# A cached-attention decode kernel: separate room for the K and V buffers, and an MLP cut into pieces between the head groups

## The chip, the cores and the metric

One core of a Trainium2 chip. The metric is the device time of one execution in microseconds, the median of several executions. All runs told here were in the fast state, with the same granted TensorE clock (0.52 on average in every kernel). A profile adds the span of one profiled execution, which lies 1 to 3 us under the median of the timed runs. In the lines of the profile PE is TensorE, PEld its weight loads, DVE VectorE, ACT ScalarE, POOL GpSimd and SP SyncE; the DMA share is the mean busy share of the core's 16 DMA engines.

## The reference

One decode step: attention over a long cache plus an MLP, both fed from the same normalised input, and a residual.

```python
# B=8, H=32, Sk=4096, Dh=128, D=576, F=4608; everything bf16
xn = _layernorm(x)
q  = (xn @ wq)                                  # 8 x 4096, 32 heads of 128
p  = softmax(einsum("bhqd,bhkd->bhqk", q, k_cache) * Dh**-0.5)
o  = einsum("bhqk,bhkd->bhqd", p, v_cache) @ wo
y  = _layernorm(xn)
m  = einsum("bsf,fd->bsd", gelu(einsum("bsd,df->bsf", y, w1) + b1), w2) + b2
return x + o + m
```

The caches K and V are 268 MB each; the four weights are 4.7 to 5.3 MB each. Everything is read once.

## The kernel before

It runs in stages: layer norms and query product; MLP; 128 groups of two heads (8 batches x 16 pairs); final product. Each group loads 2 MB of K from SP's queue and 2 MB of V from ACT's queue into three buffers each. Of the 32 blocks of keys per head, 12 are scored on PE (transposed against an identity, copied by ACT, multiplied by the query), 20 on VectorE (product with the broadcast query, four halving adds, a reduction). ACT takes the exponential, PE multiplies by V.

```python
wo_sb = const.tile([P, H, D], BF16, name="wo_sb")
nc.gpsimd.dma_start(out=wo_sb, in_=A_wo.rearrange("(h p) d -> p h d", p=P))

with tc.tile_pool(name="wq_pool", bufs=1) as wq_pool, ...:      # released before the MLP
    for ci, (d0, dn) in enumerate(d_chunks):                    # 4 blocks of 128 rows, one of 64
        nc.scalar.dma_start(out=wq_sb[:dn, ci, :], in_=A_wq[d0:d0 + dn, :])
    # ... layer norms, query product, q transposed ...

with tc.tile_pool(name="mlp_w", bufs=1) as mlp_w, ...:          # takes wq's room
    # ... w1 (5 loads), then w2, on GpSimd's queue ...
    b1T = mlp_w.tile([P, FC], BF16, name="b1T")                 # 4608 elements of 2 bytes
    nc.gpsimd.dma_start(out=b1T, in_=B_b1.rearrange("(c p) -> p c", p=P))
    for fc in range(FC):                                        # 36 x 5 matmuls, weights = w1
        ...
    # ... bias, tanh gelu, 72 matmuls with w2 moving, sum with x and b2 -> mlpx_sb

with tc.tile_pool(name="kv_pool", bufs=KV_BUFS) as kv_pool, \
     tc.tile_pool(name="kt_pool", bufs=3) as kt_pool, \
     tc.tile_pool(name="pr_pool", bufs=2) as pr_pool, ...:      # takes the MLP weights' room
    for b in range(B):
        for hg in range(NHG):
            nc.sync.dma_start(out=k_sb, in_=A_k_cache[...])     # 2 MB
            nc.scalar.dma_start(out=v_sb, in_=A_v_cache[...])   # 2 MB
            # ... PE transposes, kT copies, scores; VectorE prod, adds, reduce; exp; PV ...

# the end: normalise, then O (8 columns) stationary and wo moving
for h in range(H):
    for (n0, nn) in ncols:
        nc.tensor.matmul(acc[:, n0:n0 + nn], lhsT=On[:, h * B:(h + 1) * B], rhs=wo_sb[:, h, n0:n0 + nn], ...)
nc.vector.tensor_tensor(out=fin, in0=acc, in1=mlpx_sb, op=ALU.add)
```

The softmax here doesn't subtract the row's maximum and nothing guards it: scores larger than these inputs give would overflow.

Of the kernel before, what the change touches and what calls it, by code (L numbers as in the profile page):

```python
# [12 lines left out]
ALU = mybir.AluOpType  # L13
ACT = mybir.ActivationFunctionType
# [4 lines left out]
X_PE = int(os.environ.get("MB_X", "12"))  # L19
HG = int(os.environ.get("MB_HG", "2"))  # L20
KV_BUFS = int(os.environ.get("MB_KVB", "3"))


@with_exitstack
def kernel(
# [19 lines left out]
    assert Dh == P, Dh  # L45
    assert S % P == 0
    C = S // P
    assert F % P == 0
    FC = F // P
    d_chunks = []  # L50
    d0 = 0
    while d0 < D:
        n = min(P, D - d0)
        d_chunks.append((d0, n))
        d0 += n
    NDC = len(d_chunks)
    HD_TOTAL = H * Dh
    N512 = 512
    scale = float(Dh) ** -0.5
# [19 lines left out]
    )  # L79
    ident = const.tile([P, P], BF16, name="ident")  # L80
    make_identity(nc, ident)
    ones_f = const.tile([P, P], FP32, name="ones_f")
    nc.vector.memset(ones_f, 1.0)
    eps_col = const.tile([P, 1], FP32, name="eps_col")
# [2 lines left out]
    x8 = const.tile([B, D], BF16, name="x8")  # L87
    nc.sync.dma_start(out=x8[:], in_=x2)

    xT = const.tile([P, NDC, B], BF16, name="xT")  # L90
    yT = const.tile([P, NDC, B], BF16, name="yT")
    q8 = const.tile([B, HD_TOTAL], BF16, name="q8")
    qT = const.tile([P, H, B], BF16, name="qT")

    wo_sb = const.tile([P, H, D], BF16, name="wo_sb")
    nc.gpsimd.dma_start(out=wo_sb, in_=A_wo.rearrange("(h p) d -> p h d", p=P))

    with tc.tile_pool(name="wq_pool", bufs=1) as wq_pool, \
         tc.tile_pool(name="ln_sb", bufs=2) as ln_sb, \
         tc.tile_pool(name="ln_ps", bufs=2, space=bass.MemoryType.PSUM) as ln_ps:  # L100
        wq_sb = wq_pool.tile([P, NDC, HD_TOTAL], BF16, name="wq_sb")
        for ci, (d0, dn) in enumerate(d_chunks):
# [24 lines left out]
        y8 = const.tile([B, D], BF16, name="y8")  # L127
        layernorm(xn8, y8, "b")

        for src, dstT in ((xn8, xT), (y8, yT)):  # L130
            for ci, (d0, dn) in enumerate(d_chunks):
                tpx = ln_ps.tile([P, B], FP32, name="tpx")
                nc.tensor.matmul(tpx[:dn, :], lhsT=src[:, d0:d0 + dn], rhs=ident_b[:, :], start=True, stop=True)
                nc.vector.tensor_copy(out=dstT[:dn, ci, :], in_=tpx[:dn, :])

        nq = (HD_TOTAL + N512 - 1) // N512
        for j in range(nq):
            n0 = j * N512
            nn = min(N512, HD_TOTAL - n0)
            qps = ln_ps.tile([B, N512], FP32, name="qps")  # L140
            for ci, (d0, dn) in enumerate(d_chunks):
                nc.tensor.matmul(  # L142
                    qps[:, :nn], lhsT=xT[:dn, ci, :], rhs=wq_sb[:dn, ci, n0:n0 + nn],
                    start=(ci == 0), stop=(ci == NDC - 1),
                )
            nc.scalar.activation(out=q8[:, n0:n0 + nn], in_=qps[:, :nn], func=ACT.Copy, scale=scale)  # L146
        for h in range(H):
            tq = ln_ps.tile([P, B], FP32, name="tq")
            nc.tensor.matmul(tq[:, :], lhsT=q8[:, h * P:(h + 1) * P], rhs=ident_b[:, :], start=True, stop=True)  # L149
            nc.vector.tensor_copy(out=qT[:, h, :], in_=tq[:, :])  # L150

    sel = const.tile([B, B, P], BF16, name="sel")
    nc.vector.tensor_copy(out=sel, in_=ident_b[:, :].unsqueeze(2).to_broadcast([B, B, P]))

    mlpx_sb = const.tile([B, D], FP32, name="mlpx_sb")
    with tc.tile_pool(name="mlp_w", bufs=1) as mlp_w, \
         tc.tile_pool(name="mlp_sb", bufs=2) as mlp_sb, \
         tc.tile_pool(name="mlp_ps", bufs=1, space=bass.MemoryType.PSUM) as mlp_ps:
        w1_sb = mlp_w.tile([P, NDC, F], BF16, name="w1_sb")
        for ci, (d0, dn) in enumerate(d_chunks):  # L160
            nc.gpsimd.dma_start(out=w1_sb[:dn, ci, :], in_=B_w1[d0:d0 + dn, :])
        w2_sb = mlp_w.tile([P, FC, D], BF16, name="w2_sb")
        nc.gpsimd.dma_start(out=w2_sb, in_=B_w2.rearrange("(c p) d -> p c d", p=P))
        b1T = mlp_w.tile([P, FC], BF16, name="b1T")
        nc.gpsimd.dma_start(out=b1T, in_=B_b1.rearrange("(c p) -> p c", p=P))
        b2_bc = mlp_w.tile([B, D], BF16, name="b2_bc")
        nc.gpsimd.dma_start(out=b2_bc, in_=B_b2.partition_broadcast(B))

        hT_ps = mlp_ps.tile([P, FC, B], FP32, name="hT_ps")
        for fc in range(FC):  # L170
            for ci, (d0, dn) in enumerate(d_chunks):
                nc.tensor.matmul(  # L172
                    hT_ps[:, fc, :],
                    lhsT=w1_sb[:dn, ci, fc * P:(fc + 1) * P],
                    rhs=yT[:dn, ci, :],
                    start=(ci == 0), stop=(ci == NDC - 1),
                )
        x1 = mlp_sb.tile([P, FC, B], FP32, name="x1")
        nc.vector.tensor_tensor(  # L179
            out=x1, in0=hT_ps, in1=b1T[:, :].unsqueeze(2).to_broadcast([P, FC, B]), op=ALU.add,  # L180
        )
        t1 = mlp_sb.tile([P, FC, B], FP32, name="t1")
        nc.vector.tensor_tensor(out=t1, in0=x1, in1=x1, op=ALU.mult)
        nc.vector.tensor_scalar(out=t1, in0=t1, scalar1=0.044715, scalar2=1.0, op0=ALU.mult, op1=ALU.add)
        nc.vector.tensor_tensor(out=t1, in0=t1, in1=x1, op=ALU.mult)
        t2 = mlp_sb.tile([P, FC, B], FP32, name="t2")
        nc.scalar.activation(out=t2, in_=t1, func=ACT.Tanh, scale=GELU_C)
        nc.vector.tensor_scalar(out=t2, in0=t2, scalar1=1.0, scalar2=0.5, op0=ALU.add, op1=ALU.mult)
        hT_sb = mlp_sb.tile([P, FC, B], BF16, name="hT_sb")
        nc.vector.tensor_tensor(out=hT_sb, in0=t2, in1=x1, op=ALU.mult)  # L190

        mlp_ps2 = mlp_ps.tile([B, D], FP32, name="mlp_ps2")
        ncols = []
        c0 = 0
        while c0 < D:
            ncols.append((c0, min(N512, D - c0)))
            c0 += N512
        for fc in range(FC):
            for (n0, nn) in ncols:
                nc.tensor.matmul(  # L200
                    mlp_ps2[:, n0:n0 + nn], lhsT=hT_sb[:, fc, :], rhs=w2_sb[:, fc, n0:n0 + nn],
                    start=(fc == 0), stop=(fc == FC - 1),
                )
        tmpx = mlp_sb.tile([B, D], FP32, name="tmpx")
        nc.vector.tensor_tensor(out=tmpx, in0=x8, in1=b2_bc, op=ALU.add)
        nc.vector.tensor_tensor(out=mlpx_sb, in0=mlp_ps2, in1=tmpx, op=ALU.add)

    O_sb = const.tile([P, H, B], FP32, name="O_sb")
    Epart = const.tile([P, H, B], FP32, name="Epart")

    with tc.tile_pool(name="kv_pool", bufs=KV_BUFS) as kv_pool, \
         tc.tile_pool(name="kt_pool", bufs=3) as kt_pool, \
         tc.tile_pool(name="pr_pool", bufs=2) as pr_pool, \
         tc.tile_pool(name="e_pool", bufs=3) as e_pool, \
         tc.tile_pool(name="qb_pool", bufs=2) as qb_pool, \
         tc.tile_pool(name="ps_tp", bufs=2, space=bass.MemoryType.PSUM) as ps_tp, \
         tc.tile_pool(name="ps_sc", bufs=2, space=bass.MemoryType.PSUM) as ps_sc, \
         tc.tile_pool(name="ps_o", bufs=2, space=bass.MemoryType.PSUM) as ps_o, \
         tc.tile_pool(name="ps_qb", bufs=1, space=bass.MemoryType.PSUM) as ps_qb:

        def make_qb(b):
            qb_sb = qb_pool.tile([P, HD_TOTAL], BF16, name="qb_sb")
# [6 lines left out]
                nc.scalar.activation(out=qb_sb[:, n0:n0 + nn], in_=qb_ps[:, :nn], func=ACT.Copy)  # L229
            return qb_sb  # L230

        qb_cur = make_qb(0)
        for b in range(B):
            qb_next = None
            for hg in range(NHG):
# [9 lines left out]

                if hg == NHG // 2 and b + 1 < B:
                    qb_next = make_qb(b + 1)

                E = e_pool.tile([P, HG, C], BF16, name="E")
                kT = kt_pool.tile([P, HG, XB, 512], BF16, name="kT") if X > 0 else None  # L250
# [54 lines left out]
                    )  # L305
                for g in range(HG):
                    for c in range(C):
                        nc.tensor.matmul(  # L308
                            o_ps[:, g:g + 1], lhsT=v_sb[:, g, c, :], rhs=E[:, g, c:c + 1],
                            start=(c == 0), stop=(c == C - 1),  # L310
                        )
# [2 lines left out]
                )  # L314
            if qb_next is not None:
                qb_cur = qb_next

    with tc.tile_pool(name="fin_sb", bufs=1) as fin_sb, \
         tc.tile_pool(name="fin_ps", bufs=1, space=bass.MemoryType.PSUM) as fin_ps:
# [5 lines left out]
        On = fin_sb.tile([P, H * B], BF16, name="On")  # L325
        nc.vector.tensor_tensor(out=On, in0=O_sb[:, :, :].rearrange("p h b -> p (h b)"), in1=recip, op=ALU.mult)

        acc = fin_ps.tile([B, D], FP32, name="acc")
        ncols = []
        c0 = 0  # L330
        while c0 < D:
            ncols.append((c0, min(N512, D - c0)))
            c0 += N512
        for h in range(H):
            for (n0, nn) in ncols:
                nc.tensor.matmul(  # L336
                    acc[:, n0:n0 + nn], lhsT=On[:, h * B:(h + 1) * B], rhs=wo_sb[:, h, n0:n0 + nn],
                    start=(h == 0), stop=(h == H - 1),
                )
        fin = fin_sb.tile([B, D], BF16, name="fin")  # L340
        nc.vector.tensor_tensor(out=fin, in0=acc, in1=mlpx_sb, op=ALU.add)
        nc.sync.dma_start(out=out2, in_=fin)


# [28 lines left out]
```

## Time and profile before

| what | value |
|---|---|
| time, median of 4 runs | 1392.62 us (1391.82 to 1392.92) |
| span of the profiled execution | 1391.1 us |
| bytes moved | 559.1 MB, 402 GB/s over the span |
| busy: PE, DVE, ACT | 58%, 61%, 40% |
| chain that ended last | DMA 63%, DVE 20%, PE 11%, ACT 3% |

Bytes divided by span is the first thing to work out: 402 GB/s on average against about 426 in the steady slices. The difference is what a change at the two ends can win, 5 to 6%. The other rows say that no engine is near its limit. The lines are in the prediction.

### The profile page before, as it was taken

The page shows a single profiled execution, that of the slowest core. Times are in us where ns is not written, and L with a number is a line of the kernel's source. Part 1 is how long each engine was busy: PE and PEld are TensorE (multiplying, and loading weights), DVE is VectorE, ACT ScalarE, POOL GpSimd, SP SyncE. Part 2 cuts the span into 40 slices and gives each one's busy share as a digit, 9 for nine tenths or more (in the row PEclk, how much of TensorE's full clock was granted, in tenths as well). Part 3 has the DMA queues.
Part 4 walks back from the last instruction along what each step waited for, and adds up shares of the span by engine and source line. Part 5 has one row for each costly group of instructions (what it writes and reads, how often), then busy time and mean ns, then how long its engine had stood idle before and what let it go on. Part 6 is the DMA issues. An engine that isn't in the chain of part 4 may idle for free.

```text
span 1391.1 us, 33564 instructions
## 1 busy us (share of the span) xinstructions
PE 802.0 (58%) x14800; PEld 670.3 (48%) x14800; DVE 850.2 (61%) x1604; ACT 551.4 (40%) x1485; POOL 9.6 (1%) x17
## 2 busy tenths in 40 slices
PE   4645565756566556655556555655556555555566
PEld 1324454545454545454545454555445545445454
DVE  2026657666657576666675766666666666666663
ACT  2213343534344434443444443443435443434342
POOL 1100000000000000000000000000000000000000
PEclk9565555555555555555555555555555555555556
DMA  7849999999999999999999999999999999999991
GB/s 272 307 191 426 426 425 426 425 426 426 425 426 420 425 423 426 415 425 426 418 425 426 419 426 419 427 425 414 425 424 419 426 419 426 423 421 424 417 426 65
DMA packets 73458, 559.12 MB, mean 402 GB/s; under 512 B 4424, under 2 KB 4448, under 8 KB 6624
## 3 DMA queue, kind: packets, MB, share of 16 engines
q10 hardware_dynamic: 35472, 273.16, 47.1%
q1 hardware_dynamic: 34848, 268.46, 45.7%
q0 software_dynamic: 2992, 15.35, 3.1%
q8 instruction: 115, 1.88, 0.5%
q14 instruction: 31, 0.25, 0.0%
HBM read 556.95 MB, written 0.01 MB: 400 GB/s over the span
## 4 chain that ended last, share of the span: by engine, by line
DMA 63%; DVE 20%; PE 11%; ACT 3%; issue 1%; ACTq 1%; POOL 0%; DVEq 0%; SPq 0%
DMA k_sb<-in_A_k_cache_dram 60%; DVE prod L287 9%; DVE prod L278 9%; PE o_ps L308 6%; DMA b1T<-in_B_b_dram 2%; PE tp L260 2%; DVE sc_ps L294 2%; ACT kT L264 2%; DMA wq_sb<-in_A_wq_dram 1%; ACT E L302 1%; PE qps L142 1%; PE acc L336 1%; PE mlp_ps L200 1%; ACTq L242 1%; ACT O_sb L312 0%
## 5 line engine op out<-in xcount | busy, mean ns | idle before, releaser
L278 DVE TENSOR_TENSOR prod<-k_sb,qb_sb 128x2560 bf16<-128x2560 bf16 x256 | 370.4, 1488 | 445.0 <-DMA k_sb<-in_A_k_cache_dram 445.0
L308 PE MATMUL o_ps<-E,v_sb 128*128 128x1 bf16 x8192 | 236.2, 165 | 463.7 <-ACT E L302 463.7
L264 ACT ACTIVATE kT<-tp 128x512 bf16<-128x512 f32 x768 | 442.4, 596 | 117.7 <-PE tp L260 85.5
L308 PEld LDWEIGHTS <-v_sb 128*128 128x128 bf16 x8192 | 243.1, 105 | 488.7 <-issue 488.7
L260 PE MATMUL tp<-ident,k_sb 128*128 128x128 bf16 x3072 | 440.7, 302 | 63.7 <-ACT kT L264 31.9
L287 DVE TENSOR_TENSOR prod<-prod 128x1280 bf16<-128x1280 bf16 (+3 forms) x1024 | 401.1, 463 | 0.1
L260 PEld LDWEIGHTS <-k_sb 128*128 128x128 bf16 x3072 | 291.6, 130 | 99.2 <-issue 59.6
L302 ACT ACTIVATE E<-sc_ps 128x32 bf16<-128x32 f32 x256 | 48.1, 193 | 474.3 <-DVE sc_ps L294 474.3
L269 PEld LDWEIGHTS <-kT 128*128 128x128 bf16 x3072 | 171.0, 116 | 53.2 <-ACT kT L264 53.1
L269 PE MATMUL sc_ps<-qT,kT 128*128 128x1 bf16 x3072 | 173.1, 172 | 5.1 <-ACT kT L264 0.2
L294 DVE TENSOR_REDUCE sc_ps<-prod 128x20 f32<-128x160 bf16 x256 | 82.8, 323 | 6.1 <-PE sc_ps L269 1.8
L312 ACT ACTIVATE O_sb<-o_ps 128x2 f32<-128x2 f32 x128 | 22.2, 174 | 156.9 <-PE o_ps L308 156.9
L228 PE MATMUL qb_ps<-q,sel 8*128 8x512 bf16 x64 | 37.0, 579 | 20.7 <-ACT qb_sb L229 20.6
L229 ACT ACTIVATE qb_sb<-qb_ps 128x512 bf16<-128x512 f32 x64 | 38.4, 599 | 26.0 <-DVE prod L278 16.0
L302 ACT ACTIVATION_READ_ACCUMULATOR E<-sc_ps 128x1 f32 x256 | 47.7, 198 | 0.0
L142 PE MATMUL qps<-wq_sb,xT 128*8 128x512 bf16 (+1 forms) x40 | 14.9, 486 | 10.7 <-DMA wq_sb<-in_A_wq_dram 10.7
L179 DVE TENSOR_TENSOR x<-hT_ps,b1T 128x288 f32<-128x288 f32 x1 | 0.5, 457 | 29.8 <-DMA b1T<-in_B_b_dram 29.8
L200 PE MATMUL mlp_ps<-w_sb,hT_sb 128*8 128x512 bf16 x72 | 10.7, 317 | 10.5 <-DVE hT_sb L190 10.5
L172 PEld LDWEIGHTS <-w_sb 128*128 128x128 bf16 (+1 forms) x180 | 10.5, 106 | 7.0 <-issue 5.4
L150 DVE CAST qT<-tq 128x8 bf16<-128x8 f32 x32 | 4.1, 162 | 15.0 <-PE tq L149 14.8
L146 ACT ACTIVATE q<-qps 8x512 bf16<-8x512 f32 x8 | 4.7, 587 | 21.0 <-PE qps L142 21.0
L200 PEld LDWEIGHTS <-hT_sb 128*8 128x8 bf16 x72 | 4.6, 94 | 16.3 <-DVE hT_sb L190 10.6
(56 smaller groups left out, 73.5 us busy)
## 6 DMA issues: line engine op xcount, KB each, us to landing
k_sb<-in_A_k_cache_dram SPq DMA_DIRECT2D x128, 2048.0 KB, 18.9
v_sb<-in_A_v_cache_dram ACTq DMA_DIRECT2D x128, 2048.0 KB, 17.3
w_sb<-in_B_w_dram POOLq DMA_DIRECT2D x1, 5184.0 KB, 31.2
wo_sb<-in_A_wo_dram POOLq DMA_DIRECT2D x1, 4608.0 KB, 26.1
w_sb<-in_B_w_dram POOLq DMA_DIRECT2D x4, 1152.0 KB, 9.0
wq_sb<-in_A_wq_dram ACTq DMA_DIRECT2D x4, 1024.0 KB, 9.5
w_sb<-in_B_w_dram POOLq DMA_DIRECT2D x1, 576.0 KB, 17.6
wq_sb<-in_A_wq_dram ACTq DMA_DIRECT2D x1, 512.0 KB, 17.5
```

The source lines that it names most:

```text
L142: nc.tensor.matmul(qps[:, :nn], lhsT=xT[:dn, ci, :], rhs=wq_sb[:dn, ci, n0:n0 + nn], start=(ci == 0), stop=(ci == NDC - 1),)
L200: nc.tensor.matmul(mlp_ps2[:, n0:n0 + nn], lhsT=hT_sb[:, fc, :], rhs=w2_sb[:, fc, n0:n0 + nn], start=(fc == 0), stop=(fc == FC - 1),)
L228: nc.tensor.matmul(qb_ps[:, :nn], lhsT=sel[:, b, :], rhs=q8[:, n0:n0 + nn], start=True, stop=True)
L229: nc.scalar.activation(out=qb_sb[:, n0:n0 + nn], in_=qb_ps[:, :nn], func=ACT.Copy)
L260: nc.tensor.matmul(tp[:, t * P:(t + 1) * P], lhsT=k_sb[:, g, c, :], rhs=ident[:, :], start=True, stop=True,)
L264: nc.scalar.activation(out=kT[:, g, blk, :], in_=tp[:, :], func=ACT.Copy)
L269: nc.tensor.matmul(sc_ps[:, g, c:c + 1], lhsT=kT[:, g, blk, t * P:(t + 1) * P], rhs=qT[:, h, b:b + 1], start=True, stop=True,)
L278: nc.vector.tensor_tensor(out=prod[:, g, :, :], in0=k_sb[:, g, X:C, :], in1=qb_cur[:, h * Dh:(h + 1) * Dh].unsqueeze(1).to_broadcast([P, R ...
L287: nc.vector.tensor_tensor(out=prod[:, g, :, 0:half], in0=prod[:, g, :, 0:half], in1=prod[:, g, :, half:width], op=ALU.add,)
L294: nc.vector.tensor_reduce(out=sc_ps[:, g, X:C], in_=prod[:, g, :, 0:width], axis=mybir.AxisListType.X, op=ALU.add,)
L302: nc.scalar.activation(out=E[:, g, :], in_=sc_ps[:, g, :], func=ACT.Exp, accum_out=Epart[:, h, b:b + 1],)
L308: nc.tensor.matmul(o_ps[:, g:g + 1], lhsT=v_sb[:, g, c, :], rhs=E[:, g, c:c + 1], start=(c == 0), stop=(c == C - 1),)
```

## The change

Its intent: start reading K and V at once, by giving their buffers room that no weight holds, and do the MLP in small pieces beside the loop, so that the weights take turns in one room on the other side of the memory.

```diff
+    w1_pool = tc.alloc_tile_pool(name="w1_pool", bufs=1, side="right")   # later w2, then wo, take this room
-    wo_sb = const.tile([P, H, D], BF16, name="wo_sb")
-    nc.gpsimd.dma_start(out=wo_sb, in_=A_wo.rearrange("(h p) d -> p h d", p=P))
+    nc.sync.dma_start(out=b1T, in_=B_b1.rearrange("(p c) -> p c", p=P))
+    nc.sync.dma_start(out=b2T[:, 0:NDC_FULL], in_=B_b2[0:D_FULL].rearrange("(c p) -> p c", p=P))
+    kv_pool = ctx.enter_context(tc.tile_pool(name="kv_pool", bufs=KV_BUFS))
+    wq_pool = tc.alloc_tile_pool(name="wq_pool", bufs=1, side="right")
... the whole MLP stage is removed ...
-         tc.tile_pool(name="kt_pool", bufs=3) as kt_pool, \
-         tc.tile_pool(name="pr_pool", bufs=2) as pr_pool, \
+    with tc.tile_pool(name="kt_pool", bufs=2) as kt_pool, \
+         tc.tile_pool(name="pr_pool", bufs=1) as pr_pool, \
+        def w1_unit(j):                       # 20 matmuls, 4 of 36 blocks of F
+            for i4 in range(4):
+                for ci, (d0, dn) in enumerate(d_chunks):
+                    nc.tensor.matmul(hps[:, i4, :],
+                        lhsT=w1s[:dn, ci, :].rearrange("k (p c) -> k c p", c=FC)[:, 4 * j + i4, :],
+                        rhs=yT[:dn, ci, :], ...)
... bias, gelu -> hT_sb; w2_unit(j): 20 matmuls with w2 stationary, added into finT ...
+        for j in range(FJ):                   # FJ = 9
+            group_events.setdefault(j + 2, []).append(("w1", j))
+        group_events.setdefault(W2_ISSUE_GROUP, []).append(("w2_issue", 0))    # 11, ACT's queue
+            group_events.setdefault(W2_START_GROUP + j, []).append(("w2", j))  # 14 and on
+        group_events.setdefault(W2_START_GROUP + FJ, []).append(("wo_issue", 0))  # 23, SP's queue
...
+                if gi == 0:                   # behind the first K load
+                    for ci, (d0, dn) in enumerate(d_chunks):
+                        nc.sync.dma_start(out=w1_sb[:dn, ci, :], in_=B_w1[d0:d0 + dn, :])
... at the end: wo stationary, 160 matmuls of 8 columns; sum with finT; 5 fp32 matmuls turn it to rows ...
-                    acc[:, n0:n0 + nn], lhsT=On[:, h * B:(h + 1) * B], rhs=wo_sb[:, h, n0:n0 + nn],
+                    att_ps[:dn, ci, :], lhsT=wo_sb[:, h, d0:d0 + dn], rhs=On[:, h * B:(h + 1) * B],
```

## The prediction

> **What bounds the kernel now.** I read the slices of the page first, then the chain that ended last, then busy time by stretch at the two ends, then the timeline around the waits.
>
> ```profile
> DMA  7849999999999999999999999999999999999991
> GB/s 272 307 191 426 426 425 426 425 426 426 425 426 420 425 423 426 415 425 426 418 425 426 419 426 419 427 425 414 425 424 419 426 419 426 423 421 424 417 426 65
> ...
> HBM read 556.95 MB, written 0.01 MB: 400 GB/s over the span
> ```
>
> One slice is 34.8 us. From the fourth slice on the transfers run flat at about 426 GB/s: the loop over K and V is bound by data movement, and every engine idles in it (VectorE, the busiest, 61%). Only the first three slices and the last are below that. A change that moves no fewer bytes can win only there.
>
> ```profile
> 38.31 32.82 DMA b1T<-in_B_b_dram
> ...
> 75.49 10.71 PE mlp_ps L200 x72
> 86.22 0.76 DVE mlpx_sb L206
> ...
> 87.50 22.58 DMA k_sb<-in_A_k_cache_dram
> ```
>
> The chain in order of time (start, length, what). A 9 KB bias holds the MLP until 71 us, the second MLP product takes 10.7 us, and only then does the first K load start, at 87: the K buffers lie in the room of the MLP weights and wait until these are done with. The columns below are stretch, length, busy time and count of PE, its weight loads, DVE, ACT and POOL, granted clock, DMA share, GB/s.
>
> ```profile
> 25.00:30.00 5.00, 5.00 (x17) 1.11 (x15) 0.00 (x0) 1.72 (x3) 0.00 (x0) 1.00 0.40 151
> 30.00:35.00 5.00, 4.60 (x24) 1.54 (x23) 1.00 (x8) 2.44 (x6) 1.21 (x3) 1.00 0.00 0
> ...
> 65.00:70.00 5.00, 0.00 (x0) 0.00 (x0) 0.00 (x0) 0.00 (x0) 0.00 (x0) 0.50 0.04 7
> 70.00:75.00 5.00, 0.00 (x0) 0.00 (x0) 2.58 (x7) 0.44 (x1) 0.00 (x0) 0.50 0.00 2
> 75.00:80.00 5.00, 4.51 (x23) 1.84 (x24) 0.43 (x1) 0.00 (x0) 0.00 (x0) 0.60 0.00 0
> 80.00:85.00 5.00, 5.00 (x43) 2.34 (x40) 0.00 (x0) 0.00 (x0) 0.00 (x0) 1.00 0.00 0
> ...
> 300.00:1300.00 1000.00, 579.36 (x11239) 502.11 (x11239) 654.34 (x1210) 418.22 (x1140) 0.00 (x0) 0.50 1.01 423
> ```
>
> The reader is to see two holes in the transfers, one around 30 us (the MLP weights wait for room that the query weights hold) and one from 65 to 87. From the page, the first three slices moved (272+307+191) x 34.8 us = 26.8 MB, which 426 GB/s would move in 62.9 us instead of 104.3: **about 41 us of transfer time are lost at the front.**
>
> **What the Trainium skill says.** "DMA: Bandwidth & Descriptors", section Specifications, gives 435 GB/s as the fabric ceiling; the steady 426 of this trace is 98% of it, so I count no further speed-up of the loop. The same page, "Issuing engines are not separate DMA queues": DMAs from any engine run on the same 16 DMA engines and interleave. So moving the weights from GpSimd's queue to SP and ACT wins nothing by itself, and prefetches from both share the 426 rather than add to it; in this trace two queues with 47.1% and 45.7% share it. The same page's rules for kernel authors: a strided last dimension becomes one descriptor per element. The bias load is one such (4,608 elements of 2 bytes) and took 32.8 us from issue to landing, behind the 5.3 MB of w2 in its queue; in 65 to 70 us DMA share is 4%, so its end is latency. "ScalarE: Activation LUTs", section "Table sets: the hidden batching unit": exp and tanh share a set. The trace agrees: only two table loads of 1.28 us, before the square root and before the tanh, none before the 256 exps. So tanh amid exps should reload nothing.
>
> **The change part by part.** (1) K and V buffers get their own room, so their loads have nothing to wait for but their issue. (2) The MLP is cut into 9 pieces per product and put between head groups: w1 loads behind the first K, its pieces run in groups 2 to 10; w2 takes w1's room at group 11, pieces in groups 14 to 22; wo takes w2's room at group 23. (3) The bias gets a layout of 128 rows of 72 bytes; b2 gets 576 two-byte elements, an eighth as many as b1 before. (4) The final product is turned round: wo becomes the stationary operand. (5) kT buffers go from 3 to 2, prod buffers from 2 to 1.
>
> Transfers: the bytes stay at 559.1 MB. Before, 20.7 MB had moved by 90 us (sum of the 5 us stretches), and 538.4 MB at 423 GB/s from there end at 1362.9; the stretch 1360 to 1365 with 159 GB/s says about 1362, so the account closes. After: start 2.5 us (before, 210 GB/s in the first 5 us is a start at 2.5), plus 559.1 / 423 = 1321.7, plus 3 us for the last row block of wq and of w1, which have 64 partitions (15 to 20 us ran at 298 instead of 426, 1.5 us lost, twice), plus starvation s. End of transfers: 1327 + s.
>
> How large is s? Without any group finished, the queues hold wq 4.7, w1 5.3, three K and three V of 2.1 each: 22.6 MB, 53 us at 426. Group 0 needs wq, which shares the engines as it did with wo before (landed at 20.9, say 22), then 11 us of query products (22.7 to 33.2) and the first pieces of qT and of the broadcast query (34). VectorE then takes 2.9 us for its two products, so the first K buffer is free near 40, its V after 3.1 + 0.7 + 0.4 + 1.9 us more, near 46. Both come before the queues run dry. I take s = 3, since ACT's issue order may put a V load behind the 16 query copies.
>
> MLP pieces: 20 matmuls with weight load per group; before, 176 took 11.38 us, 65 ns each, so 1.3 us. VectorE 6 small operations, by the 0.10 to 0.24 us of small operations in the trace about 0.9. Group work is 802/128 = 6.3 us on PE and 850/128 = 6.6 on VectorE, against 4.19 MB / 426 = 9.85 us of transfer. With the pieces 7.6 and 7.5: hidden.
>
> Tail: before, 1391.1 - 1362.3 = 28.8 us. The final product was 64 matmuls in 10.8.
>
> ```profile
> 1371.79 1.85 PE L308 MATMUL o_ps<-E,v_sb 128*128 128x1 bf16 x64 [1.25 <-ACT E L302]
> ...
> 1377.22 10.77 PE L336 MATMUL acc<-wo_sb,On 128*8 128x512 bf16 x64 [2.53 <-DVE On L326]
> ```
>
> It becomes 160 matmuls with 128x128 weights and 8 columns: at the 29 ns of the PV row (1.85/64) 4.6 us, at the MLP's 65 ns 10.3; I take 7. Added: two small adds and five fp32 matmuls, about 2.5 us. Net about -1.3. Further, with two prod buffers VectorE reduces group n only after it has multiplied n+1:
>
> ```profile
> 99.09 2.90 DVE L278 TENSOR_TENSOR prod<-k_sb,qb_sb 128x2560 bf16<-128x2560 bf16 x2 [12.12 <-DMA k_sb<-in_A_k_cache_dram]
> 101.90 3.13 DVE L287 TENSOR_TENSOR prod<-prod 128x1280 bf16<-128x1280 bf16 x8
> 110.10 2.89 DVE L278 TENSOR_TENSOR prod<-k_sb,qb_sb 128x2560 bf16<-128x2560 bf16 x2 [5.07 <-DMA k_sb<-in_A_k_cache_dram]
> 112.91 3.13 DVE L287 TENSOR_TENSOR prod<-prod 128x1280 bf16<-128x1280 bf16 x8
> 115.96 0.68 DVE L294 TENSOR_REDUCE sc_ps<-prod 128x20 f32<-128x160 bf16 x2
> ```
>
> With one buffer it must reduce first, so the last group no longer carries the one before it: about -2. Tail about 25.5.
>
> Sum: 2.5 + 1321.7 + 3 + 3 + 25.5 = 1355.7 of span; the timed runs lie 1.5 above the span, so **1357 us**, 2.6% faster.
>
> **The rivals.** First, the front starves all the same: V loads sit in ACT's stream, and if they stand behind the query copies (which ran until 52 us) they come late; if in addition all K buffers are full, transfers stop for 5 to 15 us. Against it: three K and w1 are on the other queue and use the full rate. Time then 1362 to 1370. Second, the pieces break the loop: VectorE is in order, and an MLP add that waits for PE behind the last group's PV (1.9 us), then for the tanh behind kT copies, can hold up the next product. 6.6 + 0.9 + up to 4 us would exceed 9.85 by 2 us in up to 18 groups: +36, gain gone, 1390. For it: only 3.2 us of slack. Against it: VectorE sits idle for that slack at each group waiting on K, and late K reads are prefetched three deep. A part of it, 5 to 10 us, is likelier than all. Third, w2 or wo blocks K or V: 5 MB at one queue's head is 12.5 us of transfer, but transfer that must be made anyway; other queue entries go on. Cost a few us at most if a queue blocks at its issue until the room is free. Fourth, the tail may win 6 us rather than 3, if the turned product runs at 29 ns: 1353.
>
> **Range and chances.** 1350 (no starvation, fast tail) to 1367 (rivals one and two in part). The 2% line is at 1365, 8 us above my number. Faster by over 2%: 0.81; within: 0.17; slower: 0.02.
>
> **What would show it.** Right: the GB/s row at about 420 from the second slice on; first K load near 4 us; last K landing near 1330; the loop's slices unchanged in groups 2 to 23 (to about 280 us); exactly two table loads; final product under 10 us. Wrong: a slice under 400 in the first eight (rivals one to three, told apart by who holds the K issue: the DMA queue's waits naming PE's pieces or VectorE's adds is rival two); a K load that waits for a weight tile; a tail from last landing to end above 28 us.

## The result

The changed kernel took 1357.19 us (median of 8 runs, 1356.19 to 1357.71), the kernel before 1392.59 in the same rounds (13 runs, 1390.3 to 1394.34). The ratio is 0.9746, 95% interval 0.9736 to 0.9755: 2.5% faster. Ratios here are the mean time of one kernel's fast runs over that of the other's of the same rounds, so not quite the ratio of the medians. The span went from 1391.1 to 1355.2 us.

The page after, the slices (33.9 us each) and the mean rate:

```profile
DMA  9999999999999999999999999999999999999991
GB/s 354 401 426 425 434 420 426 426 418 390 427 425 426 425 427 426 425 426 426 426 426 426 426 426 425 419 424 426 423 426 420 422 425 423 426 425 416 426 424 71
HBM read 556.94 MB, written 0.01 MB: 411 GB/s over the span
```

The hole is gone. The first three slices lose (72 + 25 + 0) x 33.9 / 426 = 7.7 us where they lost 41. One new dent shows: slice 10, with 390. DMA now is 74% of the chain that ended last, DVE 3% instead of 20.

The front, in windows of the trace after (columns as in the prediction). The fourth line is the stage in which wo is loaded, the fifth a long stretch of the loop, the last two the end of the transfers:

```profile
15.00:20.00 5.00, 2.25 (x9) 0.64 (x10) 2.56 (x11) 1.55 (x2) 0.00 (x0) 1.00 1.06 377
20.00:25.00 5.00, 2.48 (x6) 0.30 (x4) 0.75 (x3) 0.88 (x2) 0.00 (x0) 1.00 0.97 302
25.00:30.00 5.00, 5.00 (x16) 1.01 (x15) 0.63 (x5) 1.17 (x2) 0.00 (x0) 1.00 1.01 425
...
300.00:310.00 10.00, 0.00 (x0) 0.00 (x0) 0.00 (x0) 0.00 (x0) 0.00 (x0) 0.50 1.05 380
...
400.00:600.00 200.00, 112.83 (x2259) 102.17 (x2256) 132.31 (x242) 81.34 (x231) 0.00 (x0) 0.50 1.01 426
...
1326.00:1328.00 2.00, 0.21 (x9) 0.12 (x5) 2.00 (x7) 0.60 (x1) 0.00 (x0) 0.50 0.52 221
1328.00:1330.00 2.00, 0.00 (x0) 0.00 (x0) 0.02 (x1) 0.00 (x0) 0.00 (x0) 0.50 0.48 205
```

Between 25 and 30 us, where the transfers of the kernel before were running out, they go at the full rate. Two dips are seen better here than on the page: the dent of slice 10 is the reading of wo, at 380 with all the DMA share taken, and in the last 8 to 9 us before the last K landing (1330.3) the rate is about half, at half the share.

The front in the timeline, first the issue of the first K load, then the first instruction of the first layer norm's square root:

```profile
3.05 0.62 SPq L297 DMA_DIRECT2D k_sb<-in_A_k_cache_dram  x1
...
14.98 1.28 ACT L136 ACT_TABLE_LOAD   x1 [14.98 <-DMA b2T<-in_B_b_dram]
```

K is issued at 3.05 us instead of about 87. But ACT, which issues the loads of wq ahead of the square root, did not get to it until a 1 KB bias had landed, at 14.4; its first instruction starts at 14.98. Neither the norm nor wq uses that bias. In the built program the transfers of SP and ACT share 8 completion semaphores in turn; the fifth load of wq came round to the one of this bias and had to wait for it, and ACT's later work stood behind that issue.

The query product ended at 42.8 us, not at the predicted 33.2, but most of that is not this wait. The last block of wq landed at 23.3, where 22 was predicted (20.9 before). From there the product took 19.5 us, where it had taken 12.3: the same 35 matmuls took 16.5 us of PE instead of 12.2, and PE did transposes and a piece of the broadcast query between them. One stretch of these matmuls before, and one after:

```profile
22.64 10.57 PE L142 MATMUL qps<-wq_sb,xT 128*8 128x512 bf16 x32
```
```profile
32.47 4.70 PE L165 MATMUL qps<-wq_sb,xT 128*8 128x512 bf16 x10
```

Why each matmul took longer was not looked into. The attention products of group 0 began at 60.2. The delay cost nothing visible: loads of w1, K and V were in hand all the while.

The tail, timeline of the trace after:

```profile
1344.16 5.36 PE L404 MATMUL att_ps<-On,wo_sb 128*128 128x8 bf16 x160 [2.44 <-DVE On L399]
...
1349.89 2.17 PE L421 MATMUL outrow<-ident_f,finT 128*8 128x128 f32 x10 [0.37 <-DVE finT L415]
...
1352.10 0.75 DVE L426 CAST fin<-outrow 8x576 bf16<-8x576 f32 x1 [2.29 <-PE outrow L421]
```

The final product takes 5.36 us instead of 10.77, and what was added behind it (two small adds, the turn to rows) takes about 2.6. From the start of that product to the end of the last VectorE instruction it was 1377.22 to 1388.78, 11.6 us, and is 1344.16 to 1352.85, 8.7.

Where the 35.9 us of span went: the last K load lands 31.9 us earlier (1330.3 against 1362.2), and from there to the end it is 24.9 us instead of 28.9.

### The profile page after: what moved, and what is told of

The parts are those of the page before. It is cut to its first block, busy times and chain, and to the rows that moved or that the text cites. A ratio compares the mean times of both kernels' runs of the same rounds, so it can differ in the third digit from the quotient of the medians.

```text
span 1355.2 us, 34075 instructions
## 1 busy us (share of the span) xinstructions
PE 778.6 (57%) x15019; PEld 688.7 (51%) x15019; DVE 867.3 (64%) x1679; ACT 529.3 (39%) x1493; POOL 1.3 (0%) x10
## 2 busy tenths in 40 slices
DMA packets 76132, 559.14 MB, mean 413 GB/s; under 512 B 5056, under 2 KB 9168, under 8 KB 9168
## 4 chain that ended last, share of the span: by engine, by line
DMA 74%; PE 17%; ACT 4%; DVE 3%; issue 1%; ACTq 1%; SPq 0%; DVEq 0%
DMA k_sb<-in_A_k_cache_dram 73%; PE tp L324 7%; PE o_ps L372 6%; ACT kT L328 4%; DVE prod L351 2%; PE mps L214 1%; DMA b2T<-in_B_b_dram 1%; PE sc_ps L333 1%; PE qb_ps L204 1%; ACTq L300 0%; DVE prod L342 0%; PE att_ps L404 0%; ACT O_sb L376 0%; DVE sc_ps L358 0%; PE mps L240 0%
## 5 line engine op out<-in xcount | busy, mean ns | idle before, releaser
L324 PE MATMUL tp<-ident,k_sb 128*128 128x128 bf16 x3072 | 435.7, 303 | 540.7 <-DMA k_sb<-in_A_k_cache_dram 475.4
L328 ACT ACTIVATE kT<-tp 128x512 bf16<-128x512 f32 x768 | 436.0, 598 | 564.1 <-PE sc_ps L333 438.6
L324 PEld LDWEIGHTS <-k_sb 128*128 128x128 bf16 x3072 | 284.9, 130 | 583.6 <-DMA k_sb<-in_A_k_cache_dram 484.7
L372 PE MATMUL o_ps<-E,v_sb 128*128 128x1 bf16 x8192 | 241.1, 166 | 4.1 <-ACT E L366 4.1
L333 PEld LDWEIGHTS <-kT 128*128 128x128 bf16 x3072 | 182.2, 118 | 13.0 <-issue 7.9
L165 PE MATMUL qps<-wq_sb,xT 128*8 128x512 bf16 (+1 forms) x40 | 19.1, 598 | 2.5 <-DMA wq_sb<-in_A_wq_dram 2.5
L214 PE MATMUL mps<-yT,w_sb 128*128 128x8 bf16 (+1 forms) x180 | 17.9, 208 | 0.0
L214 PEld LDWEIGHTS <-w_sb 128*128 128x128 bf16 (+1 forms) x180 | 16.3, 150 | 1.0
L165 PEld LDWEIGHTS <-xT 128*8 128x8 bf16 (+1 forms) x40 | 3.0, 94 | 14.2 <-issue 13.1
```

Source lines behind the costliest of these rows:

```text
L214: nc.tensor.matmul(hps[:, i4, :], lhsT=w1s[:dn, ci, :].rearrange("k (p c) -> k c p", c=FC)[:, 4 * j + i4, :], rhs=yT[:dn, ci, :], start=(c ...
L324: nc.tensor.matmul(tp[:, t * P:(t + 1) * P], lhsT=k_sb[:, g, c, :], rhs=ident[:, :], start=True, stop=True,)
L328: nc.scalar.activation(out=kT[:, g, blk, :], in_=tp[:, :], func=ACT.Copy)
L333: nc.tensor.matmul(sc_ps[:, g, c:c + 1], lhsT=kT[:, g, blk, t * P:(t + 1) * P], rhs=qT[:, h, b:b + 1], start=True, stop=True,)
L372: last_pv[0] = nc.tensor.matmul(o_ps[:, g:g + 1], lhsT=v_sb[:, g, c, :], rhs=E[:, g, c:c + 1], start=(c == 0), stop=(c == C - 1),)
```

## The experiments

The theory: the front's hole was a wait for room. K and V could not be read because weights held their place; with their own place, transfers run on, and the time is set by bytes. The rivals: that it was the bias, or the shorter tail, that won the time; that the MLP pieces cost something that the gain hides (no run leaves the MLP ahead of the loop with K and V in room of their own); and, where the trace showed dips, several reasons for those. Each run has its own kernel before in the same rounds: medians of 1391.66 in the first call (the first four runs below), 1393.13 in the second (wo and bias queues, pieces in blocks), 1391.7 in the third (the rest). The three calls ran on different chips, so differences of 1 to 2 us from the changed kernel are at the limit of what can be told: the intervals of the ratios of runs 6, 7 and 11 overlap its own.

### 1. K and V buffers under wq again

```diff
-    kv_pool = ctx.enter_context(tc.tile_pool(name="kv_pool", bufs=KV_BUFS))
-    wq_pool = tc.alloc_tile_pool(name="wq_pool", bufs=1, side="right")
+    wq_pool = tc.alloc_tile_pool(name="wq_pool", bufs=1)
...
     wq_pool.release()
+    kv_pool = ctx.enter_context(tc.tile_pool(name="kv_pool", bufs=KV_BUFS))
```

> One part undone: the K and V buffers are given the room that the query weights hold until the query product is done; all else as changed. The theory of the prediction (the gain is transfer time that used to be lost at the front, so a hole in the transfers costs its length): wq and w1, 10 MB, can move at once, 26 us with the start; K and V start when the query product ends, 33 to 43 us; so 7 to 16 us lost again, 1364 to 1373 us. Rival (the gain came from taking the MLP and its bias out of the chain, and an early K is worth little because group 0 cannot start before the query product anyway): within 2 us of the changed kernel, 1357 to 1359.

Measured: 1366.06 us (1364.96 to 1366.25), ratio 0.9819 (0.9803 to 0.9836): 8.9 us above the changed kernel. Windows of its trace:

```profile
30.00:35.00 5.00, 5.00 (x17) 1.19 (x16) 0.00 (x0) 1.76 (x3) 0.00 (x0) 1.00 0.01 2
35.00:40.00 5.00, 4.40 (x25) 1.67 (x25) 1.43 (x11) 2.84 (x5) 0.00 (x0) 1.00 0.27 52
```

A hole opens while PE works on the query product and wq cannot be given up: (424 + 374) x 5 / 426 = 9.4 us of transfer lost, and 8.9 more on the clock. A lost microsecond of transfer at the front is a microsecond of time. This is the mechanism, alone and at about a quarter of its size.

### 2. The kernel before with the new bias layout alone

```diff
-B_b1.rearrange("(c p) -> p c", p=P)
+B_b1.rearrange("(p c) -> p c", p=P)
-lhsT=w1_sb[:dn, ci, fc * P:(fc + 1) * P],
+lhsT=w1_sb[:dn, ci, :].rearrange("k (p c) -> k c p", c=FC)[:, fc, :],
```
(and the rows of w2 in the same order)

> One part alone, on the kernel before: only the bias layout with rows of 72 bytes, and w1 and w2 in the matching order; K and V still wait for the MLP. Theory: the bias landed at 71.1 but w2, which its second product needs, at 67.6, and the holes stay; 4 to 11 us gained, 1382 to 1389 us (the upper part if w2's longer rows move faster too). Rival (the 32.8 us of the bias in the chain of waits are the loss): 1357 to 1362 us.

Measured: 1391.82 us (12 runs, 1389.33 to 1395.12), ratio 1.0005 (0.9996 to 1.0015): nothing. I had expected a few microseconds, and missed. Its chain:

```profile
53.88 17.16 PE hT_ps L172 x176
75.22 11.87 PE mlp_ps L200 x72
...
88.39 22.60 DMA k_sb<-in_A_k_cache_dram
```

The bias has left the chain, but the same 176 matmuls that took 11.38 us in the kernel before now take 17.16, and sit where the bias sat. In the timeline of the kernel before:

```profile
53.60 11.38 PE L172 MATMUL hT_ps<-yT,w_sb 64*128 64x8 bf16 x176 [0.32 <-DMA w_sb<-in_B_w_dram]
```

The layout of the bias makes the weight load pick every 36th element of w1; that is 97 ns for a pair of load and matmul instead of 65. K starts at 88 us, where it started at 87. The new bias layout alone explains none of the gain; what the bias hid, made longer by the layout, came out in its place.

### 3. The old final product in the changed kernel

```diff
-for ci, (d0, dn) in enumerate(d_chunks):
-    for h in range(H):
-        nc.tensor.matmul(att_ps[:dn, ci, :], lhsT=wo_sb[:, h, d0:d0 + dn], rhs=On[...])
+for h in range(H):
+    for (n0, nn) in ncols:
+        nc.tensor.matmul(acc[:, n0:n0 + nn], lhsT=On[...], rhs=wo_sb[:, h, n0:n0 + nn])
```
(the MLP's sum is turned to rows just before)

> One part undone: the final product as before, 64 products with wo as the moving operand; the MLP sum is turned to rows ahead of it, off the path. From the two traces the stretch from On to fin is 11.7 us before and 8.8 after: 3 us slower than the changed kernel, 1360 us. Rival (the clock that the throttle grants at the end differs, so the old form would cost no more here): 1357 us.

Measured: 1361.57 us (1360.65 to 1361.95), ratio 0.9786 (0.9771 to 0.98), 4.4 above the changed kernel. The run is flawed: the turn of the MLP's sum to rows (2.2 us on PE at 1340.6) stood on the path, so that 4.4 is the product and this turn together. Run 11 mends it.

### 4. The matmuls of the first MLP pieces twice

```diff
-            for i4 in range(4):
+            for i4 in [0, 1, 2, 3] * 2:
```

> One suspected cost doubled: every first-product piece runs its 20 matmuls twice (same result). Theory of the prediction (hidden: PE 7.7 us of work in 9.85 us per group): 0 to 2 us slower, 1357 to 1359. Rival (the chain of waits in groups 2 to 10 runs through PE, VectorE and ScalarE and comes round every 9.77 us, so the stage already stands at the edge): nine times 1.87 us more, 17 us, 1374.

Measured: 1367.23 us (1366.17 to 1372.54), ratio 0.9835 (0.9815 to 0.9855), 10 above the changed kernel. My own expectation, that they stay hidden (1357 to 1359), was wrong; the measured time lies between it and the rival's 1374. Windows of its trace in the stage with the w1 pieces:

```profile
110.00:120.00 10.00, 9.18 (x150) 8.44 (x150) 5.66 (x13) 3.98 (x12) 0.00 (x0) 0.50 0.97 363
...
140.00:150.00 10.00, 7.67 (x124) 6.96 (x123) 6.30 (x18) 3.84 (x11) 0.00 (x0) 0.50 0.95 342
```

The nine additions of the bias, one per group, now come every 11.8 us; in the changed kernel every 9.88, which is the time that a group's 4.19 MB take at 425 GB/s. So the doubled pieces make this stage compute-bound. Until about 90 us the rate holds at 422 to 428, since loads in hand absorb the first 20 us of it; from 100 us on it falls to 340 to 385. The single pieces are hidden, but with less margin than I said. How long one takes shows the reason; weight loads of the w1 pieces and of the w2 pieces in the changed kernel (minimum, median and maximum in ns):

```profile
L214 PEld LDWEIGHTS <-w_sb x180: 133/158/166, 68.3 to 149.2; 128*128 128x128 bf16 x144, 64*128 64x128 bf16 x36
```
```profile
L240 PEld LDWEIGHTS <-w_sb x180: 104/104/158, 193.1 to 273.6; 128*128 128x128 bf16 x144, 128*64 128x64 bf16 x36
```

The strided loads of w1 have a median of 158 ns, the packed ones of w2 104. A w1 piece takes about 1.9 us of PE and not the predicted 1.3.

### 5. wo from GpSimd's queue

```diff
-                    nc.sync.dma_start(out=wo_sb, in_=...)
+                    nc.gpsimd.dma_start(out=wo_sb, in_=...)
```

> The wo load alone is issued from GpSimd's queue again, at the same place (group 23). In the changed kernel the transfers run at 380, 378 and 399 GB/s from 300 to 330 us while wo (rows of 1,152 bytes) comes through SP's queue, all engines idle for 28 us; in the kernel before, wo came through GpSimd's queue at 421 to 424 GB/s. Theory A (the short rows cost only in SP's queue): the lost 3 us come back, 1354 us. Theory B (rows of 1,152 bytes cost in any queue, or GpSimd's own work adds): 1357 us, the same.

Measured: 1354.54 us (1352.92 to 1354.73), ratio 0.9722 (0.9708 to 0.9735), 2.65 under the changed kernel: the best of all by its ratio (run 10 is the same within the noise). A window and the packets:

```profile
300.00:310.00 10.00, 3.33 (x77) 3.17 (x78) 2.97 (x6) 1.93 (x7) 0.00 (x0) 0.50 1.01 411
```
```profile
DMA packets 73060, 559.14 MB, mean 413 GB/s; under 512 B 5056, under 2 KB 5072, under 8 KB 6096
```

The four stretches from 300 to 340 us run at 411, 412, 414 and 424 GB/s instead of 380, 378, 399 and 415. In the changed kernel 9,168 packets were under 2 KB, here 5,072: the 4,096 rows of wo of 1,152 bytes no longer appear as such. At 426, the dent had cost (46 + 48 + 27 + 11) x 10 / 426 = 3.1 us. The queue a load is issued from did matter here. The pieces into which the load was cut changed with the queue; that they are the reason is likely, but no run changed one without the other.

### 6. The biases from GpSimd's queue

```diff
-    nc.sync.dma_start(out=b1T, in_=...)      # and the two of b2T
+    nc.gpsimd.dma_start(out=b1T, in_=...)
```

> The three bias loads are issued from GpSimd's queue, so that neither SP nor ACT waits for the b2 load at the start; the query product should end some 10 us earlier (about 33 instead of 43 us). Theory A (the transfers are the bound from the start; an earlier group 0 is worth only the dips in the first 60 us): 1355 to 1357 us. Theory B (the start of the chain of waits, b2 and then the query product, sets the end): 1347 us.

Measured: 1359.13 us (1358.96 to 1360.82), ratio 0.976 (0.9746 to 0.9773), about 2 slower than the changed kernel. No theory had the number. The chain at the front:

```profile
5.87 23.10 DMA wq_sb<-in_A_wq_dram
29.01 3.41 PE qps L165 x7
```

With no bias ahead of it, K's first load went first and shared the rate with wq, which landed at 29.0 instead of 23.3. So freeing ACT did not bring the query product forward: it ended at 46.6 instead of 42.8. The first 60 us moved 21.34 MB instead of 22.26, which is 2.2 us of transfer, the size of the loss, while the query product was 3.8 us later. So the time went with the bytes and not with the start of compute; why fewer bytes moved was not found, and this run, in which both came later, can't part the two fully.

### 7. Both queues changed

> Both of these edits together. Theory A for both: 1352 to 1354 us, the sum of the two effects, since they lie in different stages.

The edits of 5 and 6 together. Measured: 1356.27 us (1355.92 to 1357.96), ratio 0.9739 (0.9726 to 0.9752). The expectation was missed because the bias part had the other sign; with the measured parts, -2.7 and +1.9, the sum fits (1356.4).

### 8. All nine pieces at once

```diff
-            group_events.setdefault(j + 2, []).append(("w1", j))
+            group_events.setdefault(6, []).append(("w1", j))
-            group_events.setdefault(W2_START_GROUP + j, []).append(("w2", j))
+            group_events.setdefault(18, []).append(("w2", j))
```

> The MLP is not cut up: all nine first-product pieces stand in group 6, all nine second-product pieces in group 18. The PE works on the MLP for 16.8 us and about 5.4 us in one go. Theory A (the three K and V buffers hold 20 us of transfers in hand, so a single late group costs little): 1355 to 1362 us. Theory B (the slicing is what hides the MLP; a block costs its whole length): 1357 + 22 = 1379 us.

Measured: 1357.19 us (1355.63 to 1358.11), ratio 0.9739 (0.9726 to 0.9753): the same as the changed kernel. Windows around the block of w1 pieces:

```profile
110.00:120.00 10.00, 8.60 (x97) 8.00 (x97) 5.40 (x32) 2.61 (x8) 0.00 (x0) 0.50 1.01 424
120.00:130.00 10.00, 9.83 (x156) 9.29 (x154) 8.49 (x30) 3.87 (x13) 0.00 (x0) 0.50 1.00 410
```

PE is some 90% busy from 100 to 140 us, and the transfers dip no lower than 400. Three buffers of K and of V are enough to carry a block of some 17 us of extra work. Cutting the MLP finely was not needed. That it had to move under the loop is argued from the room it takes, and was not tried.

### 9 and 10. The last row block of w1 on the other half of the partitions

The reason I had for the ragged end was that the last blocks of wq and of w1 (64 rows) both load partitions 0 to 63, so that half of the DMA engines get ahead for good.

```diff
-nc.sync.dma_start(out=w1_sb[:dn, ci, :], in_=B_w1[d0:d0 + dn, :])
+nc.sync.dma_start(out=w1_sb[P - dn:, ci, :], in_=B_w1[d0:d0 + dn, :])
```
(the matching rows of y and of the matmul operands too; run 10 has wo on GpSimd's queue as well)

> In the changed kernel the transfers run at half rate (about 205 GB/s, DMA share 0.5) for the last 10 us, 1321 to 1331; in the kernel before for 4 us. Theory A: the two row blocks with 64 partitions (wq 0.52 MB, w1 0.59 MB) both land on partitions 0 to 63, that half lags by 1.11 MB / 213 GB/s = 5.2 us, and with no stop in the transfers the lag stays to the end. Here w1's last block goes to partitions 64 to 127 instead: half-rate stretch about 5 us shorter, time 2 to 3 us less, 1354.5 us. Theory B (the lag has another origin, for instance the two-byte elements at the start): half-rate stretch as long, 1357 us.

> The same together with the wo load on GpSimd's queue. If the two gains lie in different stages: 1351.5 to 1352.5 us, the best version. If the balance brings nothing: 1354.5.

Measured: 1356.84 us (1356.62 to 1357.17), ratio 0.9749 (0.9736 to 0.9763), and with wo's queue 1354.36 (1353.78 to 1354.97), ratio 0.9731 (0.9718 to 0.9745): each as without the edit. One window of the end of run 9:

```profile
1326.00:1328.00 2.00, 0.18 (x7) 0.10 (x4) 1.99 (x7) 0.60 (x1) 0.00 (x0) 0.50 0.50 213
```

The stretch at half rate is as long as before the edit. That theory falls; why half the DMA capacity runs dry 9 us early stays open.

### 11. The old final product, done properly

As run 3, but the turn of the MLP's sum to rows is made in the loop, at group 40.

> The final product as before, once more, now with the MLP sum turned to rows inside the loop (group 40), since the run with the old final product did it behind the last group, 2.2 us on the path. Theory: the turned product with its five fp32 products takes 8.7 us from On to fin and the old one, by that run's trace, 10.3: 1.5 to 2.5 us slower than the changed kernel, 1359 us. Rival: no difference, 1357 us.

Measured: 1358.44 us (1356.95 to 1359.53), ratio 0.976 (0.9747 to 0.9773): 1.25 above the changed kernel by the medians, 1.9 by the ratios (0.0014 x 1392). From its timeline:

```profile
1343.66 9.70 PE L416 MATMUL acc<-wo_sb,On 128*8 128x512 bf16 x64 [2.45 <-DVE On L406]
```

The turned product saves 4.3 us of matmuls and gives 2.6 back in the turn to rows. So it is worth 1 to 2 us of the 35, and most of the 4.4 of run 3 was the misplaced turn.

### 12. Two product buffers again

```diff
-         tc.tile_pool(name="pr_pool", bufs=1) as pr_pool, \
+         tc.tile_pool(name="pr_pool", bufs=2) as pr_pool, \
-         tc.tile_pool(name="mlp_tmp", bufs=2) as mlp_tmp, \
+         tc.tile_pool(name="mlp_tmp", bufs=1) as mlp_tmp, \
```
(and, to make room, no pad, and the fp32 identity moved to the end)

> The second prod buffer given back (room is made by one less set of small MLP buffers, and the fp32 identity is made at the end). Theory of the prediction (one buffer keeps the last group from carrying the one before it, worth 2 us of tail): 2 us slower, 1359 us, and the reduction of group n after the products of n+1 again. Rival, from the changed kernel's trace (the reduction waits there for score products that PE has put behind the next group's first transposes, so the carrying is there with one buffer too): within 1 us, 1356.5 to 1358.

Measured: 1380.09 us (5 runs, 1379.4 to 1381.32), ratio 0.9916 (0.9902 to 0.993): 23 us above the changed kernel. No theory had that. Two windows:

```profile
400.00:600.00 200.00, 117.37 (x2253) 100.98 (x2253) 128.72 (x235) 84.93 (x230) 0.00 (x0) 0.50 1.01 420
...
800.00:1000.00 200.00, 114.23 (x2230) 99.06 (x2229) 127.93 (x239) 82.46 (x226) 0.00 (x0) 0.50 1.01 417
```

The order on VectorE is the old one again. At the end, the last K landing to the last attention product is 11.4 us (1352.3 to 1363.8), as in the kernel before (1362.2 to 1373.6), against 10.4 in the changed kernel: the buffer is worth about 1 us there. The rest is in the transfers, in two parts. From 60 to 340 us, where the MLP pieces run and wo is read, they run at 408 GB/s instead of 421, which is 8 to 9 us; the edit also took one of the two sets of small MLP buffers away, and whether that, or VectorE's order with the pieces in it, is the reason was not tried. From 340 to 1300 us they run at 418 instead of 425, some 16 us, with the DMA share at 1.01 in both kernels. (A shorter end at half rate gives a few back.) In this second part the order on VectorE is not the reason, since the kernel before has it too and moves 423. The edit also moved the K and V buffers, and those of kT, the products and the broadcast query behind them, by 672 bytes in each partition. In the built programs they begin at byte 35,328 of the partition in the changed kernel and at 34,656 here, which is 32 bytes past a multiple of 64; in every other kernel of this study the start is a multiple of 64. I suspect that start for the second part, but no run moved it alone, so the cause of this run's 23 us stays open.

## Why the prediction was right

The time (1357.19 for 1357), the range and the verdict hold. Step by step:

**The bound and the mechanism.** Right. Transfers were held by room, and with room of their own they run from 3.05 us on. Run 1 took the room away and got back 9.4 us of idle transfer and 8.9 us of time; in run 6 the query product came 3.8 us later, and the 1.9 us that were lost are those of the bytes that moved later.

**The sum for the end of transfers.** The total fits better than its terms. Predicted: 2.5 + 1321.7 + 3 + 3 = 1330. Measured, with a mean loop rate of 425 GB/s: 2.5 for the start; 559.1 / 425 = 1315.6 for the bytes, 6 less than at 423; 3.2 for two dips at the front (302 and 279 GB/s, each in 5 us), which I put down to the two blocks of 64 rows, as predicted (not shown: the DMA share in them is 0.97 and 1.03, while at the end half the rate goes with half the share); 3.1 for the reading of wo; 1.8 for the stretch from 5 to 20 us at 375 to 377 GB/s; 4.1 for the end at half rate. Together 1330.3, where the last K landed. (Rates are read to 1 GB/s, so the byte term is good to about 2 us.) The faster loop and the ragged end were not foreseen and nearly cancel, which is luck. Why the loop went from 423 to 425 is not known.

**Starvation, 3 us.** Mis-sized and misplaced: no queue ran dry. The loads issued by 31 us make 22.6 MB; by the sum of the windows some 20.4 of them had moved when the next K was issued at 55.65 us, so about 5 us of transfer were still in hand. The query product was 9.6 us later than I said: 1.3 of that came before the last block of wq landed, and 8.3 are the product itself, 19.5 us instead of the 11 that I carried over from the kernel before, where nearly all of these matmuls ran back to back. (The shared semaphore, which held ACT until 14.98, I did not see either.) So the margin shrank to these 5 us, and it did no visible harm. What took the place of these 3 us in the sum are the reading of wo (3.1) and the low stretch at the front (1.8). Run 5 took away most of wo's part. For the other, b2's two-byte elements were under way, but the rate is still 377 from 15 to 20 us, after b2 had landed, so that cause is not shown.

**The MLP pieces.** Hidden, as said, but the term was mis-sized: 1.9 us of PE per piece instead of 1.3, since I took the packed load's 65 ns for the strided one. Run 4 shows that one more helping of the same work is not hidden.

**The tail.** 24.9 us for 25.5, again with terms that moved against each other. The product took 5.36, not 7, and the added work about 2.6, as predicted; the stretch shrank by 2.9, not 1.3. The other term, -2 because the last group would no longer carry the one before it, fell in its mechanism. The group of reductions in the page after:

```profile
L358 DVE TENSOR_REDUCE sc_ps<-prod 128x20 f32<-128x160 bf16 x256 | 83.9, 328 | 418.0 <-PE sc_ps L333 404.1
```

VectorE now waits 404 us in the reduction for PE's scores, where it waited in the product for K. PE, in order, starts the transposes of group n+1, which wait for that K, before the last score products of group n. So the reduction of n still comes after the landing of K n+1, and the carry is there with one buffer too. Landing to last attention product went from 11.4 to 10.4 us, so this term was worth 1, not 2.

**The rivals.** The first (starvation, 1362 to 1370) did not come: all slices of the front but the first are at 390 or more. The second (pieces break the loop) did not come, but run 4 shows it one doubling away. The third is there in small: wo's load costs 3.1 us, through its rate and not through a blocked queue. So the premise that the choice of queue makes no difference to the weights was off by the 2.65 us of run 5. The fourth, the faster tail, came.

**The signs.** First K near 4 (3.05), last landing near 1330 (1330.3), two table loads (14.98 and 58.58 us, so none at a tanh between exps), final product under 10: as said. Three slices were off: the second at 401 rather than 420, slice 10 at 390, and the first, whose 354 falls under the sign of being wrong (under 400 in the first eight). The start at 2.5 us alone would leave it at 395; the other 3.3 us are the stretch from 5 to 20 us and the dip after it, in which loads of wq, w1 and K were under way all the time, so it is not the starvation that the sign was meant to catch.

## What to carry to other kernels

When bytes over time is the bound, ask for every load what it waits for before it can be issued; a buffer placed where something else still lives is a wait that no engine's busy time shows, and a microsecond of idle transfer is a microsecond of time. Work moved under a transfer-bound loop is free up to its slack and no further, so price it from its own kind of instruction, and take the layout of its operands into account. Then look at the slices for small loads that lower the rate while the share stays full: one changed queue was worth 2.65 us here, and gives the best version (1354.54 us).

## What the Trainium skill lacked or had wrong

- "TensorE: Matmul & The Clock Gate", section "Weight-path perf modes — Fast Weight Load (FWL) and DoubleRow", allows a column step of up to 1,024 elements and gives it no price; I found no figure for one on another page. A step of 36 cost a median of 158 ns per load where the packed loads took 104, and 17.16 us instead of 11.38 for 176 matmuls in a row.
- "DMA: Bandwidth & Descriptors", section Specifications, names 512 bytes as the least transfer for line rate. Rows of 1,152 bytes from SP's queue, beside K and V, went at about 380 GB/s against 425; the same load from GpSimd's queue at 411 to 414. The section "Issuing engines are not separate DMA queues" is right that the queues share the engines, but the choice was worth 2.65 us in 1357.
- No page tells of one half of the DMA capacity running out before the other: the last 8 us before the last K landing ran at 205 to 254 GB/s with a share of 0.5 to 0.6; balancing the 64-row blocks did not change it (213 to 238).
- No page that I found tells of the time lost when a load waits for the completion of an unrelated one: here ACT came to its first activation only at 14.98 us, behind a load that waited for a 1 KB bias, because the transfers of two queues take turns on 8 semaphores.
- Not settled, and so only a question to "SBUF — State Buffer", section "Operand start alignment": with the K and V buffers, and those behind them, 32 bytes past a multiple of 64, the loop from 400 to 1300 us ran at 417 to 420 GB/s instead of 422 to 426. No run tried this alone.
